# A depthwise convolution as 16 concurrent 32x32 array tiles, with h regrouped by SBUF-to-SBUF DMA and the second matmul spread over the next batch

## The chip, the cores and the metric

One core of a Trainium2 chip runs the whole program. The metric is the device time in microseconds (us). A run that is over 1.5% above the fastest of its kernel is called slow and is left out of the ratios. Where a ratio is given, it is the mean time of one kernel's fast runs over the mean of the other's fast runs of the same rounds on the same chip, with a 95% interval; it is therefore not quite the ratio of the medians that stand beside it.

## The reference, cut to what matters

```python
# B=8 batches, H=8 heads, S=576 tokens, D=64; d_model=512, d_ff=1024
k_p, v_p = mean over groups of 8 tokens of k, v          # 72 pooled tokens
attn = softmax(q @ k_p.T / sqrt(D)) @ v_p                # (B, H, S, D)
x = attn, heads side by side                             # (B, S, 512)
h = relu(x @ w_in)                                       # (B, S, 1024)
conv_out = depthwise convolution of h over the tokens, 3 taps, one filter per channel
out = (h * sigmoid(conv_out)) @ w_out                    # (B, S, 512)
```

## The kernel before

The kernel keeps h transposed: 1024 channels are 8 blocks of 128 partitions, tokens run along the free axis. The depthwise convolution runs on the TensorE: for each block and each tap, a 128x128 matrix that is zero off its diagonal is multiplied with h, shifted by one token for each tap. Only 128 of 16,384 weights of such a matmul do work.

```python
psum = ctx.enter_context(tc.tile_pool(name="psum", bufs=4, space=bass.MemoryType.PSUM))  # 4 slots of 2 banks of PSUM, where the TensorE's results go
...
def q_prep(b, h0, n):            # transposes q on the TensorE, VectorE copies the result to qT
    ...
def scores(b, h):                # 2 matmuls on qT, then Exp on ScalarE
    ...
def mm1(b, fb):                  # h block: 8 matmuls of 128x288, then Relu (with factor 1/2) on ScalarE
    ...
def conv(b, fb):
    ps = slot("c_ps")
    for c in range(NS):                      # two halves of 288 tokens
        for kk in range(KW):                 # three taps
            o0 = PAD - 1 + c * SC + kk
            nc.tensor.matmul(out=ps[:, c, 0:SC], lhsT=dw[:, fb, kk, :],
                             rhs=hT[:, fb, o0:o0 + SC],
                             start=(kk == 0), stop=(kk == KW - 1))
    # ScalarE: tg = Tanh(ps); VectorE: t1 = tg + 1; VectorE: gT = t1 * hT   (sigmoid by way of tanh)
    ...
def mm2(b, tiles):               # per tile of 128 tokens 8 matmuls of 128x512 on gT, then copies and output DMAs
    ...
for b in range(B):
    n = b + 1                                # attention of the next batch runs inside this batch's loop
    for fb in range(n_fb + 1):
        if fb < n_fb: mm1(b, fb)
        if fb > 0:    conv(b, fb - 1)
        if fb == 0:
            k_prep(n); q_prep(n, 0, 4)       # prepares k and q ...
        elif fb == 1:
            scores(n, 0); scores(n, 1)       # ... for the scores one step later
        ...                                  # further scores, av (attn @ v), xt (transpose of x) up to step 8
    mm2(b, ...)                              # in one block at the end of the batch
```

VectorE executes its instructions in order (a place in the trace is shown below: the copy of qT starts at 176.42 us, behind a gate that waited until 175.71). It does the gate's addition and multiply, and also the copies of q, k and x that the attention's matmuls wait for.

The softmax here doesn't subtract the row's maximum and nothing guards it: scores larger than these inputs give would overflow.

Of the kernel before, what the change touches and what calls it, by code (L numbers as in the profile page):

```python
# [9 lines left out]
FP32 = mybir.dt.float32  # L10
BF16 = mybir.dt.bfloat16
# [6 lines left out]
def kernel(  # L18
# [10 lines left out]
    nc = tc.nc  # L29
# [13 lines left out]
    n_fb = d_ff // P  # L43
    KW = 3
    GRP = 32
    PAD = 2
    tok0 = [0, 128, 256, 384, S - P]

# [1 line left out]
    kv_pool = ctx.enter_context(tc.tile_pool(name="kv", bufs=2))  # L50
    q_pool = ctx.enter_context(tc.tile_pool(name="q", bufs=2))
    tree_pool = ctx.enter_context(tc.tile_pool(name="tree", bufs=2))
    qT_pool = ctx.enter_context(tc.tile_pool(name="qT", bufs=4))
    attnT_pool = ctx.enter_context(tc.tile_pool(name="attnT", bufs=12))
    r_pool = ctx.enter_context(tc.tile_pool(name="r", bufs=4))
    x_pool = ctx.enter_context(tc.tile_pool(name="x", bufs=5))
    xT_pool = ctx.enter_context(tc.tile_pool(name="xT", bufs=2))
    hT_pool = ctx.enter_context(tc.tile_pool(name="hT", bufs=2))
    gT_pool = ctx.enter_context(tc.tile_pool(name="gT", bufs=2))
    tg_pool = ctx.enter_context(tc.tile_pool(name="tg", bufs=3))  # L60
    o_pool = ctx.enter_context(tc.tile_pool(name="o", bufs=2))
# [2 lines left out]
    def slot(name):  # L64
        return psum.tile([P, 2, BANK], FP32, name=name, tag="slot")
# [8 lines left out]
    w_out_sb = const_pool.tile([P, n_fb, d_model], BF16)  # L74
    cw_rows = const_pool.tile([KW * n_fb, P], FP32)
    convw = const_pool.tile([P, KW * n_fb], FP32)
    dw = const_pool.tile([P, n_fb, KW, P], BF16)
    kz = [const_pool.tile([P, H, 2, Sp], BF16, name=f"kz{i}") for i in range(2)]
    va = [const_pool.tile([Sp, H, D + 1], BF16, name=f"va{i}") for i in range(2)]

# [29 lines left out]
        st[b] = {"k": kr, "v": vr, "q": qr}  # L110

    def tree2(raw, n):
        t1 = tree_pool.tile([Sp, n, 4, D], BF16, name="t1", tag=f"t1_{n}")
        nc.vector.tensor_tensor(out=t1, in0=raw[:, :, 0:4, :], in1=raw[:, :, 4:8, :], op=OP.add)  # L114
        t2 = tree_pool.tile([Sp, n, 2, D], BF16, name="t2", tag=f"t2_{n}")
        nc.vector.tensor_tensor(out=t2, in0=t1[:, :, 0:2, :], in1=t1[:, :, 2:4, :], op=OP.add)
        return t2

# [3 lines left out]

    def k_tree(b, raw, h0, n):
        t2 = tree2(raw, n)
        kdup = tree_pool.tile([Sp, n, 2, D], BF16, name="kdup", tag=f"kdup_{n}")
        nc.vector.tensor_tensor(
            out=kdup,
            in0=t2[:, :, 0, :].unsqueeze(2).to_broadcast([Sp, n, 2, D]),
            in1=t2[:, :, 1, :].unsqueeze(2).to_broadcast([Sp, n, 2, D]),
            op=OP.add,  # L130
        )
        ps = slot16("kT_ps")
        for i in range(n):
            nc.tensor.transpose(  # L134
                out=ps[:, 0, i * Sp:(i + 1) * Sp],
                in_=kdup[:, i].rearrange("s two d -> s (two d)"),
                identity=ident[0:Sp, 0:Sp],
            )
        src = ps[:, 0, 0:n * Sp].rearrange("p (h s) -> p h s", h=n)
        nc.vector.tensor_copy(out=kz[b % 2][0:D, h0:h0 + n, 0, :], in_=src[0:D])  # L140
        nc.vector.tensor_copy(out=kz[b % 2][D:P, h0:h0 + n, 1, :], in_=src[D:P])

    def k_prep(b):
        k_tree(b, st[b]["k"], 0, H)
# [10 lines left out]
    def q_prep(b, h0, n):  # L155
        src = st[b]["q"]
        ps = slot16("q_ps")
        for i in range(n):
            for c in range(QC):
                o0 = (i % 2) * SC + c * QP  # L160
                nc.tensor.transpose(  # L161
                    out=ps[:, i // 2, o0:o0 + QP], in_=src[:, h0 + i, c, :], identity=ident[0:QP, 0:QP]
                )
        qT = qT_pool.tile([P, n, SC], BF16, name="qT", tag=f"qT{n}")
        nc.vector.tensor_copy(  # L165
            out=qT.rearrange("d (b h) n -> d b (h n)", h=2), in_=ps[:, 0:n // 2, 0:2 * SC]
        )
        for i in range(n):
            st[b].setdefault("qT", {})[h0 + i] = qT[:, i, :]
# [61 lines left out]
    def ffn_begin(b):  # L231
        hT = hT_pool.tile([P, n_fb, S + 2 * PAD], BF16, name="hT")
        nc.gpsimd.memset(hT[:, :, 0:PAD], 0.0)
        nc.gpsimd.memset(hT[:, :, S + PAD:S + 2 * PAD], 0.0)
        st[b]["hT"] = hT
        if b % 2 == 0:
            st[b]["gT"] = gT_pool.tile([P, n_fb, 2 * S], BF16, name="gT")
        else:
            st[b]["gT"] = st[b - 1]["gT"]

    def mm1(b, fb):
        xT, hT = st[b]["xT"], st[b]["hT"]
        ps = slot("h_ps")
        for c in range(NS):
            for dc in range(n_dmc):
                nc.tensor.matmul(  # L246
                    out=ps[:, c, 0:SC],
                    lhsT=w_in_sb[:, dc, fb * P:(fb + 1) * P],
                    rhs=xT[:, dc, c * SC:(c + 1) * SC],
                    start=(dc == 0),  # L250
                    stop=(dc == n_dmc - 1),
                )
        nc.scalar.activation(  # L253
            out=hT[:, fb, PAD:S + PAD].rearrange("p (c n) -> p c n", c=NS),
            in_=ps[:, :, 0:SC],
            func=ACT.Relu,
            scale=0.5,
        )

    def conv(b, fb):  # L260
        hT, gT = st[b]["hT"], st[b]["gT"]
        ps = slot("c_ps")
        for c in range(NS):
            for kk in range(KW):
                o0 = PAD - 1 + c * SC + kk
                nc.tensor.matmul(  # L266
                    out=ps[:, c, 0:SC],
                    lhsT=dw[:, fb, kk, :],
                    rhs=hT[:, fb, o0:o0 + SC],
                    start=(kk == 0),  # L270
                    stop=(kk == KW - 1),
                )
        tg = tg_pool.tile([P, S], BF16, name="tg")
        nc.scalar.activation(  # L274
            out=tg.rearrange("p (c n) -> p c n", c=NS), in_=ps[:, :, 0:SC], func=ACT.Tanh
        )
        t1 = tg_pool.tile([P, S], BF16, name="tg1")
        nc.vector.tensor_scalar(out=t1, in0=tg, scalar1=1.0, scalar2=None, op0=OP.add)
        g0 = (b % 2) * S
        nc.vector.tensor_tensor(  # L280
            out=gT[:, fb, g0:g0 + S], in0=t1, in1=hT[:, fb, PAD:S + PAD], op=OP.mult
        )

    def mm2(b, tiles):
        gT = st[b]["gT"]
# [22 lines left out]
            in_=moe_w_in.rearrange("(c p) f -> p c f", p=P)[:, :, i * w:(i + 1) * w],  # L308
        )

    def load_w_out(i, n):
        w = n_fb // n
        nc.gpsimd.dma_start(
            out=w_out_sb[:, i * w:(i + 1) * w, :],
            in_=moe_w_out.rearrange("(c p) f -> p c f", p=P)[:, i * w:(i + 1) * w, :],
        )

    def build_conv_w():
        ps = slot("cw_ps")
# [2 lines left out]
        )  # L322
        nc.vector.tensor_copy(out=convw, in_=ps[:, 0, 0:KW * n_fb])

    def build_diag(fb):
        for kk in range(KW):
            nc.vector.tensor_scalar(
                out=dw[:, fb, kk, :],
                in0=ident,
                scalar1=convw[:, kk * n_fb + fb:kk * n_fb + fb + 1],  # L330
                scalar2=None,
                op0=OP.mult,
            )

    def build_perm():
        for g in range(P // (2 * GRP)):
# [20 lines left out]
    load_w_in(1, 4)  # L357
    load_w_in(2, 4)
    load_w_in(3, 4)
    load_w_out(0, 2)  # L360
    load_w_out(1, 2)
    for pr in range(n_pairs):
        k_prep_first(pr)
        q_prep(0, 2 * pr, 2)
        v_prep_first(pr)
        scores(0, 2 * pr)
        scores(0, 2 * pr + 1)
        if pr == 0:
            build_conv_w()
            build_diag(0)  # L370
            build_diag(1)
    for i in range(5):
        av(0, i)
    xt(0, [0, 1])
    xt(0, [2, 3])
    xt(0, [4])
    load(1)
    for fb in range(2, n_fb):
        build_diag(fb)

    for b in range(B):
        n = b + 1
        ffn_begin(b)
        for fb in range(n_fb + 1):
            if fb < n_fb:
                mm1(b, fb)
            if fb > 0:
                conv(b, fb - 1)
            if n == B:
                continue  # L390
            if fb == 0:
                k_prep(n)
                q_prep(n, 0, 4)
            elif fb == 1:
                scores(n, 0)
                scores(n, 1)
            elif fb == 2:
                v_prep(n)
                scores(n, 2)
                q_prep(n, 4, 4)  # L400
                scores(n, 3)
            elif fb == 3:
                scores(n, 4)
                scores(n, 5)
            elif fb == 4:
                scores(n, 6)
                scores(n, 7)
                if n + 1 < B:
                    load(n + 1)
            elif fb == 5:  # L410
                av(n, 0)
                av(n, 1)
            elif fb == 6:
                av(n, 2)
                xt(n, [0, 1])
            elif fb == 7:
                av(n, 3)
                av(n, 4)
            elif fb == 8:
                xt(n, [2, 3])  # L420
        slots = [[0, 1], [2, 3]] if b % 2 == 0 else [[4, 5], [6, 7], [8]]
        for s, tiles in enumerate(slots):
            mm2(b, tiles)
            if n < B and s == 0:
                xt(n, [4])


# [28 lines left out]
```

## Time and profile before

| | before |
|---|---|
| median, 2 runs | 274.79 us (274.6 to 274.97) |
| span in the profile (of a third execution, 273.04 us) | 271.3 us |
| TensorE busy | 235.3 us (87%) |
| mean granted clock | 0.985 |

In all profile lines PE is the TensorE, PEld its weight loads, DVE VectorE, ACT ScalarE and POOL GpSimd; SPq is SyncE issuing DMAs. The span runs from a program's first instruction to its last; the granted clock is the share of the TensorE's full clock that it was given.

These are lines of the page of the kernel before. In the first kind, each digit is the busy share of a fortieth of the span in tenths; PEclk is the granted clock of the TensorE in tenths of full speed, and DMA the mean busy share of the 16 DMA engines. The last two are the chain of work that ended last, as shares of the span, by engine and by line of the kernel.

```profile
PE   0047875997993999999999999999999999999994
PEclk9999997999998999999999999999999999999998
DMA  6999999999999903190319032903100320021013
...
PE 66%; DMA 21%; issue 6%; DVE 4%; POOL 1%; ACT 1%; POOLq 0%; DVEq 0%
PE o_ps L291 20%; PE h_ps L246 19%; PE c_ps L266 15%; DMA qr<-in_q_dram 7%; DMA kr<-in_k_dram 5%; DMA w_in_sb<-in_moe_w_in_dram 5%; DMA vr<-in_v_dram 4%; PE sc_ps L174 4%; PE av_ps L195 3%; PE xt_ps L222 3%; PE q_ps L161 2%; POOL qr L96 1%; DVE o L301 0%; PE kT_ps L134 0%; DVE t_2519 L114 0%
```

The DMA row holds nines until slice 14 (a slice is 6.8 us): the loads bound that part. From there on the PE row holds nines up to the last slice, and the convolution (c_ps) is 15% of the chain. How full the TensorE is shows in the windows view of the kernel before, for two stretches of two batches each. Its columns are the length of the window, the busy time of PE, PEld, DVE, ACT and POOL with instruction counts, the clock, the DMA share and GB/s.

```profile
126.60:181.60 55.00, 55.00 (x514) 39.68 (x512) 34.64 (x80) 30.54 (x53) 2.68 (x6) 1.00 0.35 66
181.60:236.60 55.00, 55.00 (x514) 39.69 (x512) 30.15 (x73) 30.55 (x53) 0.31 (x4) 1.00 0.12 44
```

The TensorE is busy for 55.00 of 55.00 us at full clock, while VectorE and ScalarE are busy for 30 to 35. A batch takes 27.5 us, all of it TensorE work.

The next lines, from the timeline of the kernel before, show the start of one batch's attention. The columns are start, duration (both us), engine, line, operation, tiles, count, and in brackets the idle time before and its releaser.

```profile
136.26 0.76 DVE L165 COPY qT<-q_ps 128x1152 bf16<-128x1152 bf16 x1
...
136.58 0.90 PE L266 MATMUL c_ps<-hT,dw 128*128 128x288 bf16 x6
...
137.32 0.65 PE L174 MATMUL sc_ps<-qT,kz_105 128*72 128x288 bf16 x4
...
137.81 1.14 PE L246 MATMUL h_ps<-xT,w_in_sb 128*128 128x288 bf16 x8
...
138.79 0.91 PE L266 MATMUL c_ps<-hT,dw 128*128 128x288 bf16 x6
```

Start to start, a convolution block (6 matmuls) takes 0.74 us, four score matmuls 0.49 us and an mm1 block 0.98 us. VectorE's copy of qT runs while the TensorE is in mm1 and the convolution.

### The profile page before, as it was taken

How to read it: one execution, taken by the hardware profiler on the slowest of the kernel's cores; microseconds unless marked ns; L12 is line 12 of the kernel's file. 1: busy time of each engine (PE TensorE's matmuls, PEld its weight loads, DVE VectorE, ACT ScalarE, POOL GpSimd, SP SyncE). 2: the span in 40 equal slices, each digit the busy share in tenths (PEclk: the TensorE clock that was granted, in tenths of full speed). 3: DMA queues.
4: the chain of work that ended last, by engine and by line, in shares of the span. 5: the costliest groups of instructions: out<-in, count | busy, mean ns of one | idle time of the engine just before them, and what ended most of it. 6: DMA issues, size and time to landing. Idle time of an engine off the chain costs nothing.

```text
span 271.3 us, 5046 instructions
## 1 busy us (share of the span) xinstructions
PE 235.3 (87%) x2049; PEld 165.5 (61%) x2049; DVE 165.7 (61%) x391; ACT 125.3 (46%) x209; POOL 29.7 (11%) x55
## 2 busy tenths in 40 slices
PE   0047875997993999999999999999999999999994
PEld 0025653874672865887588648874887488747741
DVE  3588927897964594949565936493549244942441
ACT  1014012861272721784188317840884169506720
POOL 8263010510330000100010000100000000000000
PEclk9999997999998999999999999999999999999998
DMA  6999999999999903190319032903100320021013
GB/s 159 252 165 197 174 160 143 145 188 166 176 234 165 156 1 148 49 89 0 118 39 89 0 118 77 91 0 120 39 2 0 118 77 2 0 91 66 0 48 149
DMA packets 39243, 27.22 MB, mean 100 GB/s; under 512 B 22300, under 2 KB 33460, under 8 KB 39220
## 3 DMA queue, kind: packets, MB, share of 16 engines
q0 software_dynamic: 32752, 15.09, 51.9%
q1 hardware_dynamic: 5844, 10.63, 11.1%
q10 hardware_dynamic: 624, 1.18, 1.6%
q8 instruction: 16, 0.26, 0.4%
q14 instruction: 7, 0.06, 0.1%
HBM read 32.52 MB, written 9.44 MB: 155 GB/s over the span
## 4 chain that ended last, share of the span: by engine, by line
PE 66%; DMA 21%; issue 6%; DVE 4%; POOL 1%; ACT 1%; POOLq 0%; DVEq 0%
PE o_ps L291 20%; PE h_ps L246 19%; PE c_ps L266 15%; DMA qr<-in_q_dram 7%; DMA kr<-in_k_dram 5%; DMA w_in_sb<-in_moe_w_in_dram 5%; DMA vr<-in_v_dram 4%; PE sc_ps L174 4%; PE av_ps L195 3%; PE xt_ps L222 3%; PE q_ps L161 2%; POOL qr L96 1%; DVE o L301 0%; PE kT_ps L134 0%; DVE t_2519 L114 0%
## 5 line engine op out<-in xcount | busy, mean ns | idle before, releaser
L246 PE MATMUL h_ps<-xT,w_in_sb 128*128 128x288 bf16 x512 | 77.5, 296 | 0.3 <-ACT tg L274 0.3
L291 PE MATMUL o_ps<-w_out_sb,gT 128*128 128x512 bf16 x288 | 67.0, 379 | 0.6 <-ACT tg L274 0.5
L253 ACT ACTIVATE hT<-h_ps 128x576 bf16<-128x576 f32 x64 | 41.6, 651 | 42.7 <-PE h_ps L246 42.7
L246 PEld LDWEIGHTS <-w_in_sb 128*128 128x128 bf16 x512 | 50.5, 101 | 15.2 <-issue 0.4
L266 PE MATMUL c_ps<-hT,dw 128*128 128x288 bf16 x384 | 58.8, 289 | 0.1
L182 ACT ACTIVATE attnT<-sc_ps 72x576 bf16<-72x576 f32 x64 | 37.6, 640 | 26.4 <-PE sc_ps L174 26.4
L291 PEld LDWEIGHTS <-gT 128*128 128x128 bf16 x288 | 26.9, 97 | 32.7 <-issue 3.0
L274 ACT ACTIVATE tg<-c_ps 128x576 bf16<-128x576 f32 x64 | 41.6, 650 | 10.3 <-PE c_ps L266 7.1
L266 PEld LDWEIGHTS <-dw 128*128 128x128 bf16 x384 | 37.4, 99 | 11.0 <-ACT hT L253 0.4
L299 ACT COPY o<-o_ps 128x512 f32<-128x512 f32 x16 | 9.4, 585 | 59.6 <-PE o_ps L291 59.6
L301 DVE COPY o<-o_ps 128x512 f32<-128x512 f32 x20 | 13.8, 691 | 25.7 <-PE o_ps L291 25.7
L206 DVE TENSOR_TENSOR x<-av_ps,r 128x512 bf16<-128x512 f32 x40 | 27.3, 687 | 0.6
L174 PE MATMUL sc_ps<-qT,kz_105 128*72 128x288 bf16 x64 | 13.5, 336 | 8.3 <-DVE qT L165 8.3
L161 PE MATMUL q_ps<-ident,qr 96*128 96x96 bf16 x192 | 12.6, 219 | 8.4 <-DMA qr<-in_q_dram 8.1
L222 PE MATMUL xt_ps<-perm,x 128*128 128x128 bf16 x160 | 14.5, 231 | 2.0 <-DVE x L206 1.9
L161 PEld LDWEIGHTS <-qr 96*128 96x128 bf16 x192 | 10.7, 105 | 9.0 <-DMA qr<-in_q_dram 8.4
L195 PEld LDWEIGHTS <-attnT 72*128 72x128 bf16 x320 | 14.2, 102 | 1.9 <-DVE x L206 0.6
L107 POOL DMA_DIRECT2D qr<-in_q_dram x7 | 8.3, 1189 | 61.8 <-PE sc_ps L174 57.8
L174 PE MATMUL sc_ps<-qT,kz_106 128*72 128x288 bf16 x64 | 11.6, 295 | 3.3 <-DVE qT L165 3.3
L222 PEld LDWEIGHTS <-x 128*128 128x128 bf16 x160 | 10.9, 102 | 5.8 <-DVE x L206 3.6
L174 PEld LDWEIGHTS <-kz_105 128*72 128x72 bf16 x64 | 7.7, 130 | 10.6 <-DVE qT L165 8.5
L165 DVE COPY qT<-q_ps 128x1152 bf16<-128x1152 bf16 (+1 forms) x18 | 12.4, 688 | 1.5 <-PE q_ps L161 1.1
(230 smaller groups left out, 184.2 us busy)
## 6 DMA issues: line engine op xcount, KB each, us to landing
out_dram<-o SPq DMA_DIRECT2D x36, 256.0 KB
kr<-in_k_dram POOLq DMA_DIRECT2D x7, 576.0 KB, 15.6
qr<-in_q_dram POOLq DMA_DIRECT2D x7, 576.0 KB, 8.4
vr<-in_v_dram POOLq DMA_DIRECT2D x7, 576.0 KB, 15.5
w_in_sb<-in_moe_w_in_dram POOLq DMA_DIRECT2D x4, 256.0 KB, 14.3
w_out_sb<-in_moe_w_out_dram POOLq DMA_DIRECT2D x2, 512.0 KB, 10.7
v_111<-in_v_dram ACTq DMA_DIRECT2D x2, 288.0 KB
k_110<-in_k_dram SPq DMA_DIRECT2D x2, 288.0 KB
```

The lines of the kernel that those rows point to most:

```text
L161: nc.tensor.transpose(out=ps[:, i // 2, o0:o0 + QP], in_=src[:, h0 + i, c, :], identity=ident[0:QP, 0:QP])
L174: nc.tensor.matmul(out=ps[0:Sp, c2, 0:SC], lhsT=kz[b % 2][:, h, c2, :], rhs=st[b]["qT"][h], start=True, stop=True,)
L182: nc.scalar.activation(out=at.rearrange("s (m two j) -> s two m j", two=2, j=GRP), in_=ps[0:Sp, :, 0:SC].rearrange("s two (m j) -> s two m ...
L195: nc.tensor.matmul(out=ps[:, h // 4, c:c + D + 1], lhsT=st[b]["at"][h][:, t0:t0 + P], rhs=va[b % 2][:, h, :], start=True, stop=True,)
L206: nc.vector.tensor_tensor(out=x.rearrange("p (g h) d -> p g h d", g=2), in0=y[:, :, :, 0:D], in1=r.unsqueeze(3).to_broadcast([P, 2, 4, D]) ...
L222: nc.tensor.transpose(out=y[:, pr, ii * P:(ii + 1) * P], in_=st[b]["x"][i][:, 2 * pr:2 * pr + 2, :].rearrange("p h d -> p (h d)"), identit ...
L246: nc.tensor.matmul(out=ps[:, c, 0:SC], lhsT=w_in_sb[:, dc, fb * P:(fb + 1) * P], rhs=xT[:, dc, c * SC:(c + 1) * SC], start=(dc == 0), stop ...
L253: nc.scalar.activation(out=hT[:, fb, PAD:S + PAD].rearrange("p (c n) -> p c n", c=NS), in_=ps[:, :, 0:SC], func=ACT.Relu, scale=0.5,)
L266: nc.tensor.matmul(out=ps[:, c, 0:SC], lhsT=dw[:, fb, kk, :], rhs=hT[:, fb, o0:o0 + SC], start=(kk == 0), stop=(kk == KW - 1),)
L274: nc.scalar.activation(out=tg.rearrange("p (c n) -> p c n", c=NS), in_=ps[:, :, 0:SC], func=ACT.Tanh)
L291: nc.tensor.matmul(out=ps[:, ii, :], lhsT=gT[:, fb, j * P:(j + 1) * P], rhs=w_out_sb[:, fb, :], start=(fb == 0), stop=(fb == n_fb - 1),)
L301: nc.vector.tensor_copy(out=o[:, ii, :], in_=ps[:, ii, :])
```

## The change

The intent is to use the array better. A depthwise convolution of 32 channels needs a 32x32 diagonal, and 16 such tiles fit into the 128x128 array. Four row groups take 32 channels each of one block's partitions; four column groups take four different blocks. So 16 matmuls of 32x32 are meant to run at once, and four blocks to be convolved in about the time of one. Each column group writes its own 32 partitions of the output (`out=` below), so the result comes out with its rows regrouped: h has to be brought into the same order before the gate can multiply it. 32 DMAs a batch of 36 KB, from SBUF to SBUF, do this into a new tile hB. The rows of w_out are loaded in the matching order. As a convolution now needs four blocks of h at once, half of it and all of mm2 move into the next batch's steps, and the attention is packed into 8 steps in place of 9, with its first scores directly behind the transposes of the query.

```diff
     def mm1(b, fb):
         ...                                      # matmuls and Relu as before
+        g, c = divmod(fb, NQ)
+        for r in range(NQ):
+            nc.sync.dma_start(
+                out=st[b]["hB"][QD * c:QD * (c + 1), g * NQ + r, :],
+                in_=hT[QD * r:QD * (r + 1), fb, PAD:S + PAD],
+            )
-    def conv(b, fb):
-        ...
+    def conv(b, g, c2):                          # group g of four blocks, half c2 of the tokens
+        ps = [slot("c_ps") for _ in range(2)]
+        for kk in range(KW):
+            o0 = PAD - 1 + c2 * SC + kk
+            for c in range(NQ):
+                for r in range(NQ):
+                    fb = g * NQ + c
+                    nc.tensor.matmul(
+                        out=ps[r // 2][QD * c:QD * (c + 1), r % 2, 0:SC],
+                        lhsT=dw[QD * r:QD * (r + 1), kk, fb, :],
+                        rhs=hT[QD * r:QD * (r + 1), fb, o0:o0 + SC], ...)
+        for i in range(2):
+            ...                                  # Tanh, then +1, as before, on half the tokens of two blocks
+            nc.vector.tensor_tensor(out=gT[...], in0=t1, in1=hB[...], op=OP.mult)   # the gate reads hB
     ...                                          # diagonals, w_out load and pools cut
+    def attention_step(n, step):
+        if step == 0:
+            k_prep(n)
+            q_prep(n, 0, 4)
+            scores(n, 0)                         # before: one step later, behind mm1 and conv
+            scores(n, 1)
+        ...
     for b in range(B):
+        for fb in range(n_fb):
+            mm1(b, fb)
+            if fb < 2:
+                if b > 0:
+                    conv(b - 1, 1, fb)           # group 1 of the batch before
+            elif fb in (4, 5):
+                conv(b, 0, fb - 4)
+            if b + 1 < B:
+                attention_step(b + 1, fb)
+            if b > 0:
+                if b % 2 == 1:
+                    if fb in (3, 6):
+                        mm2(b - 1, [[0, 1], [2, 3]][fb == 6])
+                elif fb in (3, 5, 7):
+                    mm2(b - 1, {3: [4, 5], 5: [6, 7], 7: [8]}[fb])
+    conv(B - 1, 1, 0)
+    conv(B - 1, 1, 1)
+    for tiles in ([4, 5], [6, 7], [8]):
+        mm2(B - 1, tiles)
```

## The prediction

> **What bounds the kernel now.** Until about 86 us the DMA engines: the page's DMA row shows 9 tenths or more in nearly every slice, and the chain of waits runs through the landings of qr, vr and kr. From 86 us the TensorE: in the windows view the stretches 126.6 to 181.6 and 181.6 to 236.6 us (two batches each, 55.0 us) have PE busy 55.00 us, ACT 30.5, DVE 30 to 35, clock 1.00. A batch costs 27.5 us of back-to-back matmuls. From the timeline, start to start: mm1 0.98 us per block (7.8 a batch), conv 0.74 per block (5.9), mm2 0.216 per matmul (7.8), attention with transposes about 5.7.
>
> **What the change does.** The conv streams 288 columns six times for each of eight blocks. Afterwards four blocks share the array: 4 calls a batch of 3 taps, 16 matmuls of 32x32 a tap. If all 16 streamed together, a call would take 3 x 0.12 us; but load-and-multiply pairs rise from 48 to 192 a batch. The Trainium skill ("TensorE: Matmul & The Clock Gate", Part 3) measured 10.6 times for 16 such tiles at 512 columns, with starts 4 ns apart; "TensorEngine Tiling (Array Packing)", Key Properties, says that a change of tiling mode drains the array. No run shows either yet. In this trace the closest two weight loads start is 15 ns; pairs in a stream never start under 29 ns apart (bound by their 65 or more columns). My estimate: 15 ns a pair, 0.72 us a call, plus 0.13 for two mode changes: 0.85 us a call, 3.4 a batch, 2.5 saved. At 30 ns a pair the conv would cost what it does now.
>
> **Added, off the TensorE.** Each batch has 32 SBUF-to-SBUF DMAs of 37 KB in 1152 B rows. Issue on SP costs about 0.4 us each (the first k loads). At the output queue's 82 ns per packet they take at most 5 us of all 16 engines a batch: free once the loads are over. The gate multiply now waits for them, and VectorE, which works in order, would carry that wait to the attention's copies. Steps 0 and 1 pack a Relu, two Tanh and two Exp on ScalarE (3.2 us at 0.65 each) against 2.7 us of PE: estimated loss 0.5 to 1 us a batch. A conv call holds two of four PSUM slots. Building the diagonals shrinks, off the critical path.
>
> **Sum.** About 6.5 batches run after the loads, each falling from 27.5 to about 25.5 us: 13 us saved. The DMA-bound start grows by up to 3 us and the tail by 1 to 2 (the last gate waits for a Relu, four DMAs and their landing). 274.8 - 13 + 2 = about 263 us, 80% range 245 to 280. Chances: faster by over 2%: 0.60; within 2%: 0.23; slower by over 2%: 0.17.
>
> **What would show each step right or wrong.**
> - A conv call's 48 matmuls start within about 0.7 us (15 ns apart). 8 ns would give some 250 us; 30 ns, no gain.
> - Two batches in the PE-bound stage take 50 to 52 us, with short PE idle before scores or conv put down to ACT tg.
> - The waits view shows DVE gT or PE o_ps waiting for the hB DMA by under 1 us a batch; several us means that the regrouping is the new bound.
> - The loads end by 86 to 90 us, as before.
>
> **What would make it wrong.** Weight loads of 32 columns that don't overlap running matmuls; row tiles that exclude each other; a DMA landing of over 4 us that blocks VectorE; or, the other way, pairs that issue every 8 ns.

## The result, and the profile after

| | before | after |
|---|---|---|
| median, 2 runs each | 274.79 us | 310.95 us (310.29 to 311.6) |
| ratio of fast runs | | 1.1316 [1.1208, 1.1424] |
| TensorE busy | 235.3 us (87%) | 231.7 us (75%) |
| mean granted clock | 0.985 | 0.917 |
| time at half clock | 10.3 us | 53.2 us |

The change made the kernel 13% slower. The time at half clock is the sum of the stretches in which the trace's clock records show 0.5; 2.0 us of it lie after the last instruction in both. Of the kernel after's other 51.2 us, 23.9 lie before batch 3, 13.7 between the batches 3 and 7, and 13.7 after that; of before's 8.3 us, 6.8, none and 1.4.

The same lines of the page of the kernel after (a slice is now 7.7 us):

```profile
PE   0068577294559869997999599979994999995674
PEclk9999999659588996999999989988998699999879
...
PE 42%; DMA 36%; DVE 8%; ACT 4%; SPq 4%; issue 4%; POOL 1%; DVEq 0%; POOLq 0%; ACTq 0%
DMA vr<-in_v_dram 19%; PE o_ps L308 18%; PE h_ps L252 14%; DMA hB<-hT 9%; DMA qr<-in_q_dram 5%; SPq L267 4%; PE sc_ps L179 4%; PE c_ps L280 3%; PE xt_ps L227 3%; DMA w_out_sb<-in_moe_w_out_dram 3%; DVE gT L294 2%; DVE x L211 2%; ACT hT L259 2%; DVE qT L170 1%; ACT tg L291 1%
```

The convolution has fallen from 15% of the chain to 3%. In its place stand the landing of the regroup DMAs (hB<-hT, 9%), their issue on SyncE (SPq L267, 4%), and VectorE's gate. The PE row has a hole once a batch, and the clock row has holes beside them. The windows view of the kernel after, for two stretches of two batches each, from the start of the key transposes of one batch to that of the second next, shows the same:

```profile
112.60:172.50 59.90, 53.31 (x807) 35.52 (x803) 36.32 (x81) 30.52 (x53) 2.70 (x6) 0.94 0.47 101
172.50:234.10 61.60, 53.61 (x799) 35.27 (x800) 30.23 (x73) 30.30 (x53) 1.50 (x5) 0.94 0.36 88
```

Two batches take 60 to 62 us in place of 55, of which the TensorE is busy for 53 to 54, at a clock of 0.94. Busy time at a lower clock includes the stretching, so it says little about the work. The phases say more. I cut each trace at the starts of the key transposes of batches 3 and 7, counted from 0:

| | to batch 3 | per batch, 3 to 7 | from batch 7 to the end | span |
|---|---|---|---|---|
| before | 108.2 us | 27.49 us | 53.1 us | 271.3 us |
| after | 112.6 us | 30.38 us | 75.7 us | 309.8 us |
| difference in the span | +4.4 | 4 x 2.89 = +11.5 | +22.6 | +38.5 |

Part of the last column is no loss: the new schedule moves about 10 us of TensorE work (one convolution group and 40 matmuls of mm2) from each batch into the next, so the end phase starts with more left to do and the first phase with less.

What fills the hole in a batch is read from the timeline of the kernel after:

```profile
171.00 0.66 ACT L259 ACTIVATE hT<-h_ps 128x576 bf16<-128x576 f32 x1
...
171.68 5.51 SPq L267 DMA_DIRECT2D hB<-hT  x8
...
171.79 0.74 PE L280 MATMUL c_ps<-hT,dw 32*32 32x288 bf16 x48
...
172.73 0.68 PE L166 MATMUL q_ps<-ident,qr 96*128 96x96 bf16 x12
...
173.71 0.46 DVE L146 COPY kz_110<-kT_ps 64x576 bf16<-64x576 bf16 x1
175.71 0.46 DVE L294 TENSOR_TENSOR gT<-tg_2686,hB 128x576 bf16<-128x576 bf16 x1 [1.54 <-DMA hB<-hT]
...
176.42 0.76 DVE L170 COPY qT<-q_ps 128x1152 bf16<-128x1152 bf16 x1
...
177.23 1.18 PE L179 MATMUL sc_ps<-qT,kz_110 128*72 128x288 bf16 x4 [3.83 <-DVE qT L170]
...
178.20 1.65 PE L252 MATMUL h_ps<-xT,w_in_sb 128*128 128x288 bf16 x6
```

Read it from top to bottom. The Relu of block 7 ends at 171.66, SyncE issues four DMAs for it and four for the next block (eight in 5.51 us). The convolution of group 1 needs block 7 and starts at once. Its gate needs block 7 in the new order and waits on VectorE for the landing until 175.71. The copy of qT is behind it in VectorE's order, so the scores are too: the TensorE stands idle for 3.83 us. Only 1.54 us of this are VectorE's wait for the landing (in brackets above); in the rest VectorE copies k, multiplies the gate and copies qT itself. Meanwhile the clock falls: the four score matmuls take 0.97 us start to start, where they took 0.49 before. Of the 4.03 us from the first issue to the gate, the issue of the first four DMAs is 2.98 (the fourth took 1.15), so the transfer is the smaller part.

This place isn't typical. The scores of the batches 3 to 7 wait for 2.55, 2.26, 3.83, 2.26 and 4.41 us, and a landing that VectorE waited for stands in front of only two of them (1.54 us here, 2.12 in batch 7). The batch after the one above has none, and its scores wait all the same:

```profile
207.71 1.17 PE L179 MATMUL sc_ps<-qT,kz_109 128*72 128x288 bf16 x4 [2.26 <-DVE qT L170]
```

The waits views, before and after, give the sum. Columns: who waited for whom, us in total, times, longest.

```profile
PE sc_ps L174 <- DVE qT L165: 11.6, 7, 4.7
```

```profile
PE sc_ps L179 <- DVE qT L170: 32.9, 13, 8.1
...
DVE gT L294 <- DMA hB<-hT: 17.7, 8, 4.3
```

The wait of the gate itself is 17.7 us in the whole run: 5.8 before batch 3, 1.5 between the batches 3 and 7, and 10.4 from batch 7 on. The wait of the scores, one engine further, has grown by 21 us. How much of this growth is the landing, passed on, is a question for an experiment.

### The profile page after: what moved, and what is told of

It reads as the page before. It is cut to its first block, busy times and chain, and to the rows that moved or that the text cites. A ratio compares the mean times of both kernels' runs of the same rounds, so it can differ in the third digit from the quotient of the medians.

```text
span 309.8 us, 7741 instructions
## 1 busy us (share of the span) xinstructions
PE 231.7 (75%) x3183; PEld 150.0 (48%) x3201; DVE 162.1 (52%) x372; ACT 123.2 (40%) x209; POOL 32.4 (10%) x61
## 4 chain that ended last, share of the span: by engine, by line
PE 42%; DMA 36%; DVE 8%; ACT 4%; SPq 4%; issue 4%; POOL 1%; DVEq 0%; POOLq 0%; ACTq 0%
DMA vr<-in_v_dram 19%; PE o_ps L308 18%; PE h_ps L252 14%; DMA hB<-hT 9%; DMA qr<-in_q_dram 5%; SPq L267 4%; PE sc_ps L179 4%; PE c_ps L280 3%; PE xt_ps L227 3%; DMA w_out_sb<-in_moe_w_out_dram 3%; DVE gT L294 2%; DVE x L211 2%; ACT hT L259 2%; DVE qT L170 1%; ACT tg L291 1%
## 5 line engine op out<-in xcount | busy, mean ns | idle before, releaser
L252 PE MATMUL h_ps<-xT,w_in_sb 128*128 128x288 bf16 x512 | 85.3, 312 | 1.4
L308 PE MATMUL o_ps<-w_out_sb,gT 128*128 128x512 bf16 x270 | 70.3, 392 | 9.1 <-DVE gT L294 4.3
L252 PEld LDWEIGHTS <-w_in_sb 128*128 128x128 bf16 x512 | 53.4, 106 | 23.8 <-issue 3.1
L308 PEld LDWEIGHTS <-gT 128*128 128x128 bf16 x288 | 28.2, 100 | 38.6 <-issue 7.3
L291 ACT ACTIVATE tg<-c_ps 128x576 bf16<-128x576 f32 x64 | 38.1, 654 | 5.6 <-PE c_ps L280 4.8
L318 DVE COPY o<-o_ps 128x512 f32<-128x512 f32 x20 | 13.8, 691 | 30.8 <-PE o_ps L308 30.8
L179 PE MATMUL sc_ps<-qT,kz_109 128*72 128x288 bf16 x64 | 14.7, 358 | 18.6 <-DVE qT L170 18.6
L280 PE MATMUL c_ps<-hT,dw 32*32 32x288 bf16 x1536 | 25.1, 303 | 2.9 <-DVE x L211 2.7
L179 PE MATMUL sc_ps<-qT,kz_110 128*72 128x288 bf16 x64 | 14.1, 343 | 14.3 <-DVE qT L170 14.3
L280 PEld LDWEIGHTS <-dw 32*32 32x32 bf16 x1536 | 14.5, 89 | 16.2 <-issue 10.1
L166 PE MATMUL q_ps<-ident,qr 96*128 96x96 bf16 x192 | 13.6, 229 | 10.6 <-DMA qr<-in_q_dram 9.7
L210 DVE RECIPROCAL r<-av_ps 128x8 f32<-128x8 f32 x40 | 7.5, 197 | 26.8 <-PE av_ps L200 26.8
L166 PEld LDWEIGHTS <-qr 96*128 96x128 bf16 x192 | 11.6, 111 | 11.5 <-DMA qr<-in_q_dram 10.1
L227 PEld LDWEIGHTS <-x 128*128 128x128 bf16 x160 | 12.3, 108 | 10.1 <-issue 7.0
```

The lines of the kernel that those rows point to most:

```text
L166: nc.tensor.transpose(out=ps[:, i // 2, o0:o0 + QP], in_=src[:, h0 + i, c, :], identity=ident[0:QP, 0:QP])
L179: nc.tensor.matmul(out=ps[0:Sp, c2, 0:SC], lhsT=kz[b % 2][:, h, c2, :], rhs=st[b]["qT"][h], start=True, stop=True,)
L227: nc.tensor.transpose(out=y[:, pr, ii * P:(ii + 1) * P], in_=st[b]["x"][i][:, 2 * pr:2 * pr + 2, :].rearrange("p h d -> p (h d)"), identit ...
L252: nc.tensor.matmul(out=ps[:, c, 0:SC], lhsT=w_in_sb[:, dc, fb * P:(fb + 1) * P], rhs=xT[:, dc, c * SC:(c + 1) * SC], start=(dc == 0), stop ...
L280: nc.tensor.matmul(out=ps[r // 2][QD * c:QD * (c + 1), r % 2, 0:SC], lhsT=dw[QD * r:QD * (r + 1), kk, fb, :], rhs=hT[QD * r:QD * (r + 1), ...
L291: nc.scalar.activation(out=tg, in_=ps[i][:, :, 0:SC], func=ACT.Tanh)
```

## The experiments

The theory after the result (A): the gate's wait for the landing, passed on by VectorE's order, is the main loss. The rivals: (B) the new schedule alone, in which the scores follow directly on the query's transposes, and mm2 is spread out; (C) the 16-tile convolution itself costs the TensorE more than it seems; (D) the issue of the DMAs on one queue, or their traffic, is too slow.

Kernels that read hT in place of hB multiply the wrong rows: their results are **wrong**. They take the wait away without a race. Unless it is said otherwise, a kernel's result was correct.

### 1. Take the regroup's wait away, then its DMAs (wrong results on purpose)

e1_gate_hT, against the kernel after; the DMAs are still issued, nobody reads them, and the TensorE's instructions are in the same order:

```diff
-                in1=hB[:, f0:f0 + 2, c2 * SC:(c2 + 1) * SC],
+                in1=hT[:, f0:f0 + 2, PAD + c2 * SC:PAD + (c2 + 1) * SC],
```

> Wrong result on purpose: the gate multiplies by hT in its old place, so nothing computes with hB, but all 256 regrouping DMAs are still issued; the order of instructions on the TensorE is the same as in the changed kernel. Theory W (VectorE waits in order for the hB landing, and holds back qT and x, so the TensorE idles and its clock drops): 265 to 285 us, no DVE wait for hB, TensorE idle before scores under 1 us a batch. Rival S (the new schedule, with conv holding two of four PSUM slots and mm2 spread out, is what stalls): still 300 us or more. Rival D (the DMA traffic lengthens the loads): still above 300 us.

e2_no_dma has the same edit, and takes the DMAs out of mm1 and the tile hB as well:

```diff
-        g, c = divmod(fb, NQ)
-        for r in range(NQ):
-            nc.sync.dma_start(out=st[b]["hB"][...], in_=hT[...])
```

> Wrong result on purpose: as the run that gates with hT, but the regrouping DMAs are not issued either. Theory W: within 4 us of the run that gates with hT but keeps the DMAs. Rival D: lower than that run by more than 5 us, most of it before 90 us. Rival S: still 300 us or more. If W and nothing else is at work, this should be near 255 to 270 us, since the TensorE has 3.3 us less work a batch than before.

Measured: e1 289.29 us, ratio to before 1.0569 [1.0496, 1.0642]; e2 282.34 us, 1.0303 [1.0243, 1.0363]. The wait for the landing is worth 1.1316 - 1.0569 = 7.5% of the time before, some 21 us. The presence of the DMAs is worth another 2.7%, 7 us; of that, 5.6 us are gained by the start of batch 3 (107.0 against 101.4 us), while the DMA engines still have the loads to carry. So the landing is behind over half of the loss. Both runs missed what A expected, though: e1 lies above 265 to 285 us, and e2 saves 7 us more where at most 4 were expected, most of it early, as D expected of the DMAs' traffic.

And the path that A names carries the smaller part. In e1's trace no gate waits for a landing, yet the scores wait for nearly as long as the 32.9 us of the kernel after:

```profile
PE sc_ps L179 <- DVE qT L170: 27.4, 12, 9.7
```

In e1's batches 3 to 7 it is 2.25 to 2.35 us each. The 22.6 us between the two spans divide by phases into 5.6 up to batch 3, 4.3 from batch 3 to 7 (1.1 us a batch), and 12.8 from batch 7 on, where the last matmuls of mm2 wait for gates. So the landing is paid for mostly at the end, and only in small part through the scores, whose wait falls by 5.5 us. And e2, with a free regroup and the cheap convolution, is still 3% slower than before: something else is in the schedule or the convolution.

### 2. The new schedule with the old convolution

e3_spread_128 keeps before's convolution of 128x128 matmuls, without any regrouping, in after's schedule:

```diff
+            if fb > 0:
+                conv(b, fb - 1)                  # before's conv, one block
+            elif b > 0:
+                conv(b - 1, n_fb - 1)
             if b + 1 < B:
                 attention_step(b + 1, fb)        # and mm2 spread, as in after
```

> Correct result: the kernel before, with its 128x128 conv and no regrouping, in the changed kernel's schedule (second matmul of a batch spread over the next batch's steps, attention in eight steps). Theory W: 270 to 282 us, as before within 3%. Rival S, if the spreading itself stalls the TensorE: 290 us or more.

e4_mm2_block is the kernel after with mm2 in one block:

```diff
-            if b > 0:
-                if b % 2 == 1:
-                    if fb in (3, 6): ...
+            if b > 0 and fb == 3:
+                for tiles in [[0, 1], [2, 3]] if b % 2 == 1 else [[4, 5], [6, 7], [8]]:
+                    mm2(b - 1, tiles)
```

> Correct result: the changed kernel, with the second matmul of a batch in one block at step 3 of the next batch, not spread over steps 3 to 7. Theory W: about as the changed kernel, 304 to 318 us. Rival S: faster than the changed kernel by 8 us or more.

Measured: e3 289.85 us, 1.0569 [1.0505, 1.0632]; e4 308.28 us, 1.1254 [1.1184, 1.1324]. Rival B is real too: the schedule alone costs 5.7%, with no DMA and no small tile in it. Spreading mm2 is not what costs: e4 and the kernel after can't be told apart by their intervals. In e3's trace, the matmuls of four batches start 12.5 us later than their nominal spacing adds up to (1.4 us in before; section 5 has the spacings); 9.2 us of this lie between a query transpose and the first scores, 2.14 us idle in each batch, with no landing to wait for.

The pair e2 and e3 also has a reading for C: the schedule is the same and only the convolution differs, and the 16-tile one is 2.7% faster. It is no burden, but its gain is small.

### 3. Move the attention back by a step

e5_scores_later puts the first scores where they were before, behind an mm1 and a convolution:

```diff
         if step == 0:
             k_prep(n)
             q_prep(n, 0, 4)
-            scores(n, 0)
+        elif step == 1:
+            scores(n, 0)
+            ...
```

The further steps follow one later, with the issue of the next loads among them; the last two hold two items each. So the edit moves the whole attention, not the first scores alone.

> Correct result: the changed kernel with the attention moved back by about one step, as it was before: the first scores no longer stand right behind the query transposes that feed them, but behind the next block of mm1 and a conv call. Theory Q (the new schedule's cost, 15 us with the 128x128 conv, is this wait of the TensorE for the qT copy, once a batch): 288 to 298 us, and no TensorE idle before the first scores of over 1 us a batch. If the cost is in the spread mm2 or the later tail: 305 us or more.

e6_later_gate_hT is e5 with e1's edit (wrong), e7_later_128 is e3 with e5's edit, each word for word as shown above:

```diff
# e6, against e5
-                in1=hB[:, f0:f0 + 2, c2 * SC:(c2 + 1) * SC],
+                in1=hT[:, f0:f0 + 2, PAD + c2 * SC:PAD + (c2 + 1) * SC],
# e7, against e3
         if step == 0:
             k_prep(n)
             q_prep(n, 0, 4)
-            scores(n, 0)
+        elif step == 1:
+            scores(n, 0)
+            ...
```

> Wrong result on purpose: the same later attention, and the gate reads hT (DMAs still issued), so that neither wait is there. If Q and the wait for the landing are separate and add up: 270 to 278 us. If they are one and the same wait (moving the scores hides both): within 4 us of the run with later scores alone.

> Correct result: the 128x128 conv in the changed kernel's schedule, with the later attention. Theory Q: back to 272 to 280 us, where the same without the move took 290. Rival (spreading mm2 over the next batch costs by itself): 285 us or more.

Measured: e5 287.88 us, 1.0487 [1.0403, 1.0571]; e6 276.95 us, 1.0075 [1.0002, 1.0148]; e7 279.09 us, 1.0156 [1.0088, 1.0224]. Moving the attention back by one step is worth 23 us of the 36 (e5 against after: 7.7 up to batch 3, 9.5 from 3 to 7, 6.1 from 7 on), and 11 us where no DMA is involved (e7 against e3). In the other direction, the landing's wait costs 21 us where the scores follow directly (after against e1), and 11 us where they don't (e5 against e6). The timeline of e5 shows the scores of a batch:

```profile
165.02 0.68 PE L179 MATMUL sc_ps<-qT,kz 128*72 128x288 bf16 x4 [0.53 <-DVE qT L170]
```

The scores now wait for 0.53 us here, and for 8.5 us in the run where it was 32.9. In e5 the batches 3 to 7 take 28.01 us each, and the half clock lasts for 24.7 us in the run, against 53.2; none of it lies between the batches 3 and 7.

### 4. The same schedule without any DMA, and the old schedule with the new convolution (wrong on purpose)

e17_later_no_dma is e6 with the DMAs and hB taken out by the edit shown for e2. It is what the change could give at best in this schedule, if the regrouping were free. e18_old_schedule puts the 16-tile convolution with a free regroup (e2's) into before's loop:

```diff
             # e18, against before's loop
             if fb < n_fb:
                 mm1(b, fb)
-            if fb > 0:
-                conv(b, fb - 1)
+            if fb in (5, 6):
+                conv(b, 0, fb - 5)
+            elif fb == 8:
+                conv(b, 1, 0)
+                conv(b, 1, 1)
```

> Wrong result on purpose: later attention, the gate reads hT, and no regrouping DMAs at all: the 16-tile conv with its regrouping made free, in the new schedule. If landing traffic adds to the rest as it did before the scores were moved (7 us): 268 to 273 us, which would leave 6 to 11 us of gain over the 128x128 conv in the same schedule (279 us), of the 26 us of TensorE time that the conv saves on paper. If 255 to 262 us: the saving is all there once the regrouping is gone.

> Wrong result on purpose: the 16-tile conv with the regrouping made free, in the schedule of the kernel before (attention in nine steps, the second matmul at the end of each batch, no lag). If the saved conv time is real time: 252 to 262 us. If other engines' latencies fill it again, because the TensorE has less to do while it waits for them: 265 to 275 us, with the batches after 108 us at 25.5 to 27.5 us and TensorE idle or held up by 1.5 to 3 us a batch.

Measured: e17 271.76 us, 0.9884 [0.9797, 0.9972]; e18 280.58 us, 1.0226 [1.015, 1.0303]. At the 2% bound both verdicts are "unclear", but neither interval holds 1. e17 lies in its 268 to 273 us. Both ranges named for e18 (252 to 262, and 265 to 275 us) were missed: it is slower than before. By phases it takes 113.6 us to batch 3, 27.98 us a batch and 50.8 at the end (before: 108.2, 27.49, 53.1), so it gains nothing per batch. Its windows view shows that the TensorE isn't full any more, for the first time in this schedule:

```profile
163.00:218.00 55.00, 51.33 (x798) 34.59 (x800) 29.75 (x74) 30.28 (x52) 1.54 (x6) 1.00 0.23 56
```

So the gain on paper is lost even with no regrouping and no new schedule. e18 isn't quite the convolution alone, though: the second group's calls stand together at the end of the batch.

### 5. Where the convolution's gain goes

A batch of before has about 27.15 us of TensorE work when each matmul is taken at its nominal spacing, the start-to-start time in an unbroken stream: 64 of mm1 at 0.122 us, 48 of the convolution at 0.123, 36 of mm2 at 0.216, and 5.7 us for the attention. A call of the 16-tile convolution takes 0.76 us in e17 where nothing holds it up (0.094 on entering behind mm1, 0.444 from its first start to its last, 0.222 to the next matmul), so a batch of the kernel after has 24.30. The 2.85 us saved are real on the TensorE. (My expectation of e17 speaks of 26 us in the run, 3.75 a batch; that left out most of the time of entering and leaving a call.) Yet e17 takes 27.74 us a batch, and e7, with the old convolution, 28.72. One microsecond of the 2.85 arrives.

In e17's four batches the matmuls start 13.8 us later than nominal (6.3 in e7, 1.4 in before), spread over many short waits: 2.4 us from a convolution call to the scores, 1.6 from mm1 to the scores, 1.5 from the transposes of x to mm1, 1.2 each between scores, between transposes of x and from the scores to mm1, and others. None of them is long enough to stand out in the waits view. One apparent wait was none: ten of 144 matmuls of mm2 are missing from e17's trace in these batches, which looks like 2.2 us of waiting in mm2.

A rival explanation was that ScalarE holds the PSUM slots too long (a call of the convolution takes two of four slots until their Tanh is done). e9_short_tanh and e10_short_exp are e6 with a Tanh, or an Exp, of 32 of every 288 columns (wrong twice over):

```diff
-            nc.scalar.activation(out=tg, in_=ps[i][:, :, 0:SC], func=ACT.Tanh)
+            nc.scalar.activation(out=tg[:, :, 0:32], in_=ps[i][:, :, 0:32], func=ACT.Tanh)
# e10: the same for the Exp of the scores
+        nc.scalar.activation(out=at[32 of each 288 columns], in_=ps[0:Sp, :, 0:32], func=ACT.Exp, ...)
```

Both write into tiles that are filled once at the start, so that nothing unwritten is read.

> Wrong result on purpose: the run with later attention and the gate reading hT (277 us), with each Tanh cut to 32 of its 288 columns a bank, so that a conv call gives its two PSUM slots back about 0.5 us a Tanh sooner and ScalarE has about 4 us less work a batch. Theory P (with the waits for the landing and for qT gone, what still eats the saved conv time is that PSUM slots come back at ScalarE's pace, two Tanh behind each conv call): 255 to 266 us, steady batches of 25 to 26 us where they take 27.8. Rival (the TensorE stream itself, mode changes included, takes the time): within 3 us of 277.

> Wrong result on purpose: the same base, with the Exp cut instead of the Tanh (to 32 of 288 columns a bank), which takes as much work off ScalarE but leaves the Tanh and the conv's two slots. Theory P in the narrow form (the conv's own two slots): within 4 us of 277. If it is ScalarE's load in the crowded steps, whoever makes it: as much faster as the run with the short Tanh.

Measured: e9 272.3 us, 0.9915 [0.9831, 0.9999]; e10 275.18 us, 0.9987 [0.9911, 1.0063]. e6 has 1.0075. I had expected 255 to 266 us of e9, and missed: its batches 3 to 7 take 27.18 us, against 27.78 in e6. By the ratios, cutting the Tanh is worth 1.6% (4.4 us) and the Exp 0.9% (2.4 us); for e10 the intervals overlap with e6's, and the runs were on another chip than e6's. Both cuts together were not tried.

e8_later_lag gave each convolution a step more of room behind its mm1:

```diff
-            if fb < 2: ... conv(b - 1, 1, fb)
-            elif fb in (4, 5): conv(b, 0, fb - 4)
+            if fb in (1, 2): ... conv(b - 1, 1, fb - 1)
+            elif fb in (5, 6): conv(b, 0, fb - 5)
```

mm2 starts from step 4 in place of 3.

> Correct result: later attention, and each conv call one step later as well (steps 5, 6 and the next batch's 1, 2; mm2 from step 4), so that a regrouping DMA has about one step more to land before the gate wants it. Theory W: faster than the run with later attention alone by 5 us or more, 275 to 288 us. If the DMA wait is already hidden, or its cost is the tail and the load stage: within 3 us of it.

Measured: 287.49 us, 1.0458 [1.0363, 1.0554], not different from e5. The miss says that by then the gate's wait inside the batch was hidden (between the batches 3 and 7 e5 takes only 0.23 us a batch more than e6); what e5 still loses against e6 lies elsewhere. By phases it lies at the end: from batch 7 to the end, e5 takes 69.6 us and e6 60.3.

### 6. The end of the run: one queue

The last batch has no attention to hide anything behind, and SyncE has 32 DMAs to issue. This is the timeline of the kernel after, near the end:

```profile
291.06 3.08 SPq L267 DMA_DIRECT2D hB<-hT  x4
...
295.74 0.46 DVE L294 TENSOR_TENSOR gT<-tg_4857,hB 128x576 bf16<-128x576 bf16 x1 [3.97 <-DMA hB<-hT]
...
296.25 9.63 PE L308 MATMUL o_ps<-w_out_sb,gT 128*128 128x512 bf16 x36 [4.29 <-DVE gT L294]
```

The last matmuls wait for 4.29 us for the last four DMAs, which leave in sequence behind their predecessors. e11_later_tail tried to fill this wait, by holding mm2 of batch 6 back until after the last convolution. e12_even did the same, set the convolution at steps 0, 2, 5 and 7, the one of step 0 behind the attention's preparation, and mm2 at steps 4, 6 and 7:

```diff
# e12 alone
+            if fb == 0: attention_step(b + 1, 0)
-            if fb < 2: conv(b - 1, 1, fb)
-            elif fb in (4, 5): conv(b, 0, fb - 4)
+            if fb in (0, 2): conv(b - 1, 1, fb // 2)
+            elif fb in (5, 7): conv(b, 0, (fb - 5) // 2)
# e11 and e12: no mm2 in the last batch's steps; instead, after the last conv
+    for tiles in ([0, 1], [2, 3]):
+        mm2(B - 2, tiles)
     for tiles in ([4, 5], [6, 7], [8]):
         mm2(B - 1, tiles)
```

> Correct result: the changed kernel with later attention (288 us), and in the last batch the second matmul of the batch before kept back until after the last conv calls, to fill the wait for the last block's landing. If the wait for the landing at the end costs what the trace of the later-attention run shows (about 5 us of idle TensorE before the last mm2, and the slow clock after it): 278 to 284 us. If not: within 2 us of 288.

> Correct result: the best version that these runs point to. Later attention, the last batch as in the run with the filled end, the copies of k and q ahead of the waiting gate on VectorE, and the conv calls spread over steps 0, 2, 5 and 7 so that no step has two Tanh, two Exp and a Relu. Estimate 268 to 278 us: about as the kernel before, perhaps up to 2% faster, since the load stage and the landing traffic remain.

Measured: e11 293.74 us, 1.0687 [1.0613, 1.0761]; e12 288.43 us, 1.0505 [1.0436, 1.0573]. Both missed: e11 lost 6 us against e5. The timeline of e11 has the reason:

```profile
245.74 21.18 SPq L267 DMA_DIRECT2D hB<-hT  x32
...
267.11 0.46 DVE L294 TENSOR_TENSOR gT<-tg,hB 128x576 bf16<-128x576 bf16 x1 [6.62 <-DMA hB<-hT]
...
270.47 16.22 PE L308 MATMUL o_ps<-w_out_sb,gT 128*128 128x512 bf16 x59 [9.41 <-DVE o L318]
```

Without mm2 between them, the Relus of the last batch come faster than SyncE can issue: 32 DMAs take 21.18 us, 0.66 us each. And the matmuls held back as filling didn't run in the wait, because their output copy stood behind the waiting gate in VectorE's order. The filling was put behind the very wait that it was to fill.

e13_two_queues, e14_later_two_queues and e15_even_two_queues issue half of the DMAs from GpSimd, from batch 3 on, in the kernel after, in e5 and in e12:

```diff
+            eng = nc.gpsimd if b >= 3 and r >= 2 else nc.sync
-            nc.sync.dma_start(
+            eng.dma_start(
```

> Correct result: the changed kernel, with half of the regrouping DMAs of batches 3 to 7 issued from GpSimd, nothing else changed. Theory I (the regrouping is bound by how fast one queue can issue: 0.59 to 0.66 us a DMA, 32 a batch, 19 to 21 us, so a block's last DMA leaves late and the last batch, which has only 10 to 17 us of TensorE work, waits for the queue): 292 to 302 us, most of it won in the last two batches. Theory L (the time from issue to landing is what counts, about 2 us, whoever issues): within 3 us of the changed kernel.

> Correct result: later attention and the two issuing queues together. Theory I: 278 to 283 us, against 288 with one queue; the last two batches fall from 70 us towards the 60 us that they take when the gate does not wait at all. Theory L: 285 to 291 us.

> Correct result: the evened-out version (288 us, whose batches before the last pair are the shortest of all, 27.2 us) with the two issuing queues. Its trace with one queue shows the last batch's 32 DMAs leaving over 21.5 us while the TensorE is done with that batch's other work in 11. Theory I: 274 to 280 us. Theory L: 286 to 290 us.

| | one queue (ratio) | two queues | end phase, one to two queues |
|---|---|---|---|
| after, e13 | 1.1316 | 305.31 us, 1.1153 [1.1086, 1.1219] | 75.7 to 67.1 us |
| e5, e14 | 1.0487 | 283.96 us, 1.0359 [1.031, 1.0409] | 69.6 to 63.8 us |
| e12, e15 | 1.0505 | 280.44 us, 1.0199 [1.0135, 1.0263] | 73.4 to 65.5 us |

D holds for the end phase: a second queue shortens it by 6 to 9 us. (The phases come from one profile each; e13's is of the fastest of its four runs, and by the ratios it gains 1.6%, 4.5 us.) Nothing was gained per batch between 3 and 7 (30.38 to 31.11, 28.01 to 28.27, 27.18 to 27.34 us). By the medians all three missed what they expected, e13 clearly (292 to 302 us), e14 and e15 by 1 us or less. In e15 SyncE took 0.78 us for each of its 16 of the last batch; the median of one was 0.563, but two took 1.6 us:

```profile
243.06 12.52 SPq L268 DMA_DIRECT2D hB<-hT  x16
```

e16_last_batch is e15 with a quarter of the last batch's DMAs from ScalarE, and the last output copies on ScalarE:

```diff
+            if b == B - 1 and r == 1:
+                eng = nc.scalar
...
-            if ii:
+            if ii or tail:                       # tail: the mm2 calls after the last conv
                 nc.scalar.copy(out=o[:, ii, :], in_=ps[:, ii, :])
```

> Correct result: as the evened-out version with two queues, and in the last batch a quarter of the DMAs from ScalarE's queue, with the last output copies on ScalarE too, so that they do not stand behind a waiting gate on VectorE. Theory I: 2 to 6 us faster than two queues, 270 to 277 us: about the kernel before.

Measured: 282.89 us, 1.0292 [1.023, 1.0354]; a miss, the end phase stayed at 65.5 us. e15 is the fastest version with the 16-tile convolution that gives the right result, and it is slower than before (its interval lies above 1, though at the 2% bound the verdict is "unclear"). No version with the right result that beats before was found.

## Why the prediction was wrong

The steps of the prediction that failed are "each falling from 27.5 to about 25.5 us", with its "estimated loss 0.5 to 1 us a batch", and "the tail by 1 to 2": a batch took 30.38 us, and the end phase grew by 22.6 us. What each had wrong follows.

The kernels above form a ladder from before to after. It gives every part of the loss one number, in this order of undoing; another order shares it out differently, because the first scores' position and the landing wait overlap. The first two rungs bundle edits (e7 also delays mm2; e17 also sets the convolution calls at other steps), and e17 was measured on another chip than e5 to e7, each against before on its own chip.

| rung | ratio to before | step |
|---|---|---|
| before | 1 | |
| new schedule, scores one step later, old convolution (e7) | 1.0156 | +1.6% |
| 16-tile convolution, free regroup (e17) | 0.9884 | -2.7% |
| DMAs issued, not waited for (e6) | 1.0075 | +1.9% |
| gate waits for them (e5) | 1.0487 | +4.1% |
| attention a step earlier, first scores directly behind the query's transposes (after) | 1.1316 | +8.3% |

**The bound.** Right: full TensorE from about 86 us on, 27.5 us a batch.

**The convolution's cost.** The sum was right: a call of 48 pairs takes 0.67 us start to start, shown above between 171.79 and the key transposes at 172.46. The time added on entry to a convolution behind mm1 is 94 ns a case in e17, where 65 were assumed. Per batch, 4 x 0.76 us = 3.0 in place of 5.9: 2.9 us saved, 2.5 predicted. That "15 ns a pair" gave this sum is in part luck. The pairs of a tap start 3 to 4 ns apart in the first two taps of a call and 8 ns in the third; the time goes between the taps, whose first starts lie 0.134 and 0.185 us apart, and on entering and leaving the call. The prediction's own test ("8 ns would give some 250 us") would have misled.

**From saved work to saved time.** Wrong, and the deepest error. "6.5 batches ... each falling from 27.5 to about 25.5 us: 13 us saved" assumed that the rest of the schedule would stay hidden. Removing the DMAs and the wait entirely (e17) leaves 27.74 us a batch. The reading that fits: a TensorE that is busy for 55.00 of 55.00 us hides the other engines' latencies behind its own work, and taking work out exposes them; e17's many short waits agree, but no run shows it for each. The whole gain of the 16 tiles was 7 us (e7 to e17, and e3 to e2), not 13 and not the 20 that 2.85 us a batch over 7 batches would have made.

**"Estimated loss 0.5 to 1 us a batch".** Wrong, in its path and its size. I had read the new steps 0 and 1 only for the load on ScalarE, and overlooked that step 0 now holds the query's transposes and the first scores together, with VectorE's copies of k and qT between them. The TensorE idles there for 2.3 to 4.4 us in each of the batches 3 to 7, where before had no wait of over 0.9 us; most of it stays in e1, without any wait for a landing (2.25 to 2.35 us), and in e3, without any DMA (2.14 us). It goes when the attention moves back by a step (e5: 0.5 to 1.1 us).

**The wait for the hB DMAs "under 1 us a batch".** About right inside the batches 3 to 7, where taking it away is worth 1.1 us a batch (e1), and wrong at the two ends: 5.6 us up to batch 3 and 12.8 from batch 7 on, where the sum allowed for up to 3 and for 1 to 2. It had been named under what would make the prediction wrong ("a DMA landing ... that blocks VectorE"), and sized without following it there.

**The clock.** The TensorE runs at half clock for 53.2 us in the run against 10.3, in part at these waits. The Trainium skill ("TensorE: Matmul & The Clock Gate", HAM oscillation) says that idle gaps of over about 3.4 us make the clock fall to half. The place shown agrees, with 3.83 us idle, then scores at 0.97 in place of 0.49 us; but here shorter gaps were enough too: the clock also fell at the waits of 2.55 and 2.26 us (scores at 116.11 and 207.71), and behind 8 of the 15 waits of 2.14 to 2.35 us in e1, e2 and e3. An estimate from the two totals: at most (53.2 - 10.3) / 2 = 21 us of the loss are the clock's, if the TensorE had had work all of that time; 17 us of the difference lie before batch 3, where the loads bound it for a good part. No run separates the clock's share from the idle time's.

**"The tail by 1 to 2 us."** Wrong in size. The end phase grew by 22.6 us, about 10 of it shifted work; without the wait for the landings (e1) it is 12.8 us shorter. I had taken 0.4 us for an issue on SyncE; the median was 0.588, and 0.66 to 0.69 in a series, so that the last batch's 32 DMAs take about 21 us to issue (21.18 in e11). The first phase grew by 4.4 us, although the schedule had moved work out of it ("up to 3 us" predicted).

What stays open is the exact share of each of the small waits that hold e17 at 27.74 us a batch. e9 and e10 show only that neither the Tanh nor the Exp alone is the main one; the copies of x, q and k on VectorE were not tried one by one. Nor is it shown why the phase up to batch 3 swings from 97.7 (e17) to 113.6 us (e18).

## What to carry to other kernels

Where one engine is full, the saving from thinning it out must be read from a schedule, not from the sum of its busy time: here 1 us a batch arrived of 2.85. Before a matmul moves up to what feeds it, look at what the feeding engine does in between: here VectorE's copies left the TensorE idle for over 2 us a batch, and moving the attention back by one step undid most of the loss. A wait chain in one timeline can mislead: the place shown has the landing in it, yet the run without that wait (e1) kept 27.4 of the 32.9 us. Many small DMAs on one queue cost issue time (0.588 us each here), and the place to look for it is where nothing else is left to do.

## What the Trainium skill lacked or had wrong

- "DMA: Bandwidth & Descriptors", Issuing engines are not separate DMA queues, says that issuing on several engines saves only the sequencer's time, "which is usually small relative to the DMA itself". Here that time mattered at the end of the run: 32 SBUF-to-SBUF DMAs of 36 KB took 21.18 us to issue from SyncE (0.66 us each), and a second issuing engine shortened the end phase by 6 to 9 us. The page has no issue time measured on this chip for a DMA of this kind (a section on another chip gives sequencer cycles for "previous generations"); the runs show 0.507 us at least and 0.588 in the median.
- "TensorE: Matmul & The Clock Gate", Part 3, gives 10.6 times for 16 tiles of 32x32 at 512 columns, from starts 4 ns apart. The starts agree here (3 to 4 ns in the first two taps of a call, 8 in the third). What the page lacks is the cost of going on with new weights: the three taps of a call, 288 columns each, took 0.67 us start to start, and 0.76 with the entry. The convolution went from 5.9 to 3.0 us a batch, 1.9 times; at most 4 could be had, as each 128x128 matmul did the useful work of four tiles, so this is not to be compared with the page's ratio.
- "TensorEngine Tiling (Array Packing)", Key Properties, says that a change of tiling mode drains the TensorE, without a number. Entering the 16-tile calls behind mm1 took 94 ns more than nominal a case (e17), and from a call's last start to the next matmul it was 219 ns at least, where 288-column matmuls start 122 ns apart.
- "TensorE: Matmul & The Clock Gate", HAM oscillation, names idle gaps of over about 3.4 us. Here the half clock also followed waits of 2.14 to 2.55 us, though not each of them (none at 147.50 us in the kernel after, 2.26 us idle). What it doesn't have is where such gaps come from here: not from a matmul's own DMA, but from VectorE's copies, which the matmul needs.
